# A fused attention block: five exponentials per slot of the main output projection, kept in 23 more tiles, and four PSUM banks shared by that projection and the maxima

## The chip, the cores and the metric

The kernel runs on one core of a Trainium2 chip. The metric is the time of one execution on the device in microseconds (us). TensorE (PE) multiplies and writes PSUM banks; VectorE (DVE), ScalarE (ACT) and GpSimd (POOL) work on SBUF and PSUM; SyncE (SP) issues most DMA transfers, in program order.

## The reference

```python
x = A_x                                   # 1 x 2048 x 512, fp32
xn = (x - mean) / sqrt(var + 1e-5)        # over the last axis
q, k, v = xn @ wqkv                       # 32 heads of 16
p = softmax(q @ k.T * 16 ** -0.5)         # per head, 2048 x 2048
s = (p @ v, heads side by side) @ wo
h = max(xn @ w1 + b1, 0) ** 2             # 1792 wide
g = silu(h @ w2 + b2)
return x + s * g
```

## The kernel before

Every fp32 product of the dense parts is made of three matmuls of split values (high times high, high times low, low times high). The attention is 512 slots. A unit is four heads with 512 queries; unit u takes slots 16u to 16u+15, one block of 128 keys (kb) in each. A slot makes one score tile for each of the four heads, and these go through an exp on ScalarE; two slots later four matmuls of them with v (32 output rows each, L401) add into the unit's bank `po`.

Score matmuls and the dense ones use 64 rows of the TensorE array, so two run side by side, one on each row half. In a slot one half has the dense work of the MLP or of a projection, and the other the maxima and the score matmuls; the next slot swaps the halves. The text calls one matmul on each half a round.

A unit's exps need its row maxima first, since they are subtracted inside the score matmul (two extra rows of the q tile hold the shift). So each unit's scores are made twice: 64 matmuls L317 whose tiles VectorE reduces (L324), 24 slots ahead of the unit, and later those for the exps (L1201). When the 64 are done, `max_end` notes a slot from which the shift is formed (`late`, six slots later); `shift` makes it (L368 to L371), stores it (L377, one slot later) and loads it into the rows of the q tile (L392).

PSUM has three banks for exps (`se`), three for maxima (`pm_t`), one for dense work (`pd_t`) and one for `po`. `tile` pools hand them out in turn: who writes a bank again waits for the reader of what was there. Exp results go to a ring of 17 tiles `pt`.

A unit's output leaves in steps counted in slots (`evac`; EVAC_LAST for units 29 on): the row sums are loaded into another shape (L419), inverted, stored (L428), loaded back to all rows (L433, `hl<-r_d`), GpSimd multiplies and splits (L439), and four stores (L448) put it into `on_d`, from which the projection loads its input (L677, `oc<-on_d`).

The output projection has two parts. The main part (`wo_part`, slots 454 to 485) makes 16 tiles of 128 x 512 over heads 0 to 23, two slots each, nine dense matmuls on each half; a tile is multiplied by g, x is added, and the sum goes to `sp_d` or stays in SBUF. The last part (`wo_last`, slots 486 to 510) does heads 24 to 31 for 12 tiles, three dense matmuls a slot, beside the exps of units 30 and 31; slot 502 has no dense work. Slot 494 starts on the tiles that need unit 29's output, slot 503 on those of unit 30. The four tiles that need unit 31 are made after slot 511 (`unit_final`). From slot 486 on (LAST_MAX) no maxima are left and exps take turns in the banks of both pools.

The order on TensorE is as the code writes it. Within a slot a string gives what stands beside the dense matmuls on the other half, `s` an exp's and `m` a maximum's:

```python
order = "s" * len(ex) if spare else {0: "smsmsmsm", 1: "smsmssm"}[k]
if not spare and post is None:
    if k == 0:
        order = "msmsmsms"
```

SyncE's transfers are issued in one queue in the order of the slots in which `later(n, ...)` places them; one that waits holds all behind it.

## Time and profile before

| | |
|---|---|
| time, median of 3 runs | 1630.25 us (1628.72 to 1631.37) |
| the profiled execution | 1627.99 us, span 1626.2 us |
| mean granted TensorE clock | 0.999 |
| TensorE busy | 1610.3 us of the span (99%) |
| VectorE, ScalarE, GpSimd busy | 84%, 73%, 32% |
| DMA | 208.16 MB, 128 GB/s over the span |

A row of an engine's timeline has the start in us, the time from the start of its first instruction to the end of its last, engine, line, operation, output<-inputs, tile and number of merged instructions; in brackets the idle time ahead of it and what ended that. A matmul's own time overlaps the next one's. SPq is SyncE's queue: the time at which it issues a transfer. A row of the windows' view has the stretch, then its length and for PE, PE's weight loads, DVE, ACT, POOL the busy time (and instructions), then the granted clock, the DMA engines' busy share and GB/s.

### The profile page before, as it was taken

The page shows a single profiled execution, that of the slowest core. Times are in us where ns is not written, and L with a number is a line of the kernel's source. Part 1 is how long each engine was busy: PE and PEld are TensorE (multiplying, and loading weights), DVE is VectorE, ACT ScalarE, POOL GpSimd, SP SyncE. Part 2 cuts the span into 40 slices and gives each one's busy share as a digit, 9 for nine tenths or more (in the row PEclk, how much of TensorE's full clock was granted, in tenths as well). Part 3 has the DMA queues.
Part 4 walks back from the last instruction along what each step waited for, and adds up shares of the span by engine and source line. Part 5 has one row for each costly group of instructions (what it writes and reads, how often), then busy time and mean ns, then how long its engine had stood idle before and what let it go on. Part 6 is the DMA issues. An engine that isn't in the chain of part 4 may idle for free.

```text
span 1626.2 us, 36026 instructions
## 1 busy us (share of the span) xinstructions
PE 1610.3 (99%) x13656; PEld 936.1 (58%) x13656; DVE 1362.1 (84%) x2359; ACT 1188.9 (73%) x2349; POOL 520.5 (32%) x547
## 2 busy tenths in 40 slices
PE   8999999999999999999999999999999999999998
PEld 6899665556545654664466456545654565445543
DVE  6486888888888888888888888888888888887744
ACT  7212777777777777877777777777777777777786
POOL 6436667133113310321133112311331133226421
PEclk9999999999999999999999999999999999999999
DMA  8877556434343333434343334423542252247564
GB/s 297 235 236 233 175 162 157 127 96 128 81 103 96 103 88 90 127 87 110 83 119 93 85 87 130 112 68 83 141 112 67 70 155 78 55 126 210 188 179 150
DMA packets 163565, 208.16 MB, mean 128 GB/s; under 512 B 59168, under 2 KB 79136, under 8 KB 161824
## 3 DMA queue, kind: packets, MB, share of 16 engines
q1 hardware_dynamic: 163104, 205.33, 44.6%
q8 instruction: 108, 1.77, 0.5%
q14 instruction: 65, 0.53, 0.1%
q10 hardware_dynamic: 288, 0.52, 0.1%
HBM read 148.64 MB, written 55.56 MB: 126 GB/s over the span
## 4 chain that ended last, share of the span: by engine, by line
PE 98%; DVE 1%; DMA 0%; issue 0%; SPq 0%; DVEq 0%; ACT 0%; ACTq 0%
PE po L401 31%; PE pd_t L255 20%; PE pm_t L317 16%; PE se L1201 14%; PE pd_t L223 7%; PE pm_t L1077 4%; PE pd_t L1077 1%; PE se L1047 1%; PE se L981 1%; PE se L317 1%; PE pm_t L1163 0%; PE pd_t L1047 0%; DVE mx L324 0%; DMA xt<-in_A_x_dram 0%; PE pm_t L1201 0%; PE po L981 0%
## 5 line engine op out<-in xcount | busy, mean ns | idle before, releaser
L324 DVE TENSOR_REDUCE mx<-pm_t 128x1 f32<-128x512 f32 x1927 | 1197.3, 684 | 166.9 <-PE pm_t L317 74.0
L1213 ACT ACTIVATE pt<-se 128x512 f32<-128x512 f32 x1996 | 1035.5, 614 | 252.8 <-PE se L1201 210.4
L317 PE MATMUL pm_t<-ka,qm 64*128 64x512 f32 x1927 | 769.6, 420 | 0.0
L1201 PE MATMUL se<-qe,ka 64*128 64x512 f32 x1996 | 673.0, 396 | 0.3 <-ACT pt L1213 0.3
L401 PE MATMUL po<-pt,v 128*32 128x512 f32 x4096 | 545.3, 604 | 0.2 <-DVE tsm L795 0.2
L317 PEld LDWEIGHTS pm_t<-ka,qm 64*128 64x128 f32 x1927 | 338.3, 184 | 237.0 <-DVE mx L324 225.5
L1201 PEld LDWEIGHTS se<-qe,ka 64*128 64x128 f32 x1996 | 337.2, 184 | 18.1 <-ACT pt L1213 1.7
L255 PEld LDWEIGHTS pd_t<-xc,w1s 64*128 64x128 f32 x2352 | 292.0, 186 | 82.2 <-issue 82.2
L255 PE MATMUL pd_t<-xc,w1s 64*128 64x256 f32 x2352 | 332.2, 288 | 0.0
L255 PE MATMUL pd_t<-w2t,hT 64*128 64x512 f32 x1080 | 300.6, 410 | 0.0
L255 PEld LDWEIGHTS pd_t<-w2t,hT 64*128 64x128 f32 x1080 | 179.0, 184 | 83.2 <-issue 75.5
L555 POOL TENSOR_TENSOR r<-r 128x512 f32<-128x512 f32 x56 | 58.2, 1039 | 370.3 <-ACT r L552 370.3
L401 PEld LDWEIGHTS po<-pt,v 128*32 128x32 f32 x4096 | 81.0, 108 | 159.9 <-issue 136.8
L574 POOL TENSOR_TENSOR u<-u,b_t 128x512 f32<-128x512 f32 x16 | 20.6, 1289 | 320.2 <-ACT u L573 286.3
L324 DVE TENSOR_REDUCE mx<-se 128x1 f32<-128x512 f32 x121 | 77.9, 686 | 26.0 <-PE se L317 26.0
L439 POOL TENSOR_TENSOR ot<-ot,hl 128x512 f32<-128x512 f32 x30 | 38.6, 1286 | 173.9 <-DMA hl<-r_d 132.7
L223 PE MATMUL pd_t<-wot,oc 64*128 64x512 f32 x336 | 90.2, 405 | 0.4 <-issue 0.3
L552 ACT ACTIVATE r<-pd_t,b_t 128x256 f32<-128x256 f32 x112 | 47.0, 470 | 57.0 <-PE pd_t L255 53.8
L223 PEld LDWEIGHTS pd_t<-wot,oc 64*128 64x128 f32 x336 | 58.4, 184 | 46.9 <-ACT pt L1213 12.6
L1077 PE MATMUL pm_t<-xT,wr_t 64*128 64x512 f32 x408 | 73.8, 388 | 0.0
L97 POOL TENSOR_TENSOR hT<-r,hT 128x512 fp32r<-128x512 f32 x56 | 72.3, 1291 | 4.7
L223 PE MATMUL pd_t<-w2t,hT 64*128 64x512 f32 x264 | 68.8, 393 | 0.0
(134 smaller groups left out, 1148.4 us busy)
## 6 DMA issues: line engine op xcount, KB each, us to landing
w1s<-w_d SPq DMA_DIRECT2D x196, 256.0 KB
qm<-q_d SPq DMA_DIRECT2D x384, 32.0 KB
ka<-k_d SPq DMA_DIRECT2D x96, 128.0 KB
qe<-q_d SPq DMA_DIRECT2D x384, 32.0 KB
q_d<-hl SPq DMA_DIRECT2D x16, 512.0 KB
g<-g_d SPq DMA_DIRECT2D x32, 256.0 KB
k_d<-hl SPq DMA_DIRECT2D x15, 512.0 KB
hl<-r_d SPq DMA_DIRECT2D x30, 256.0 KB
```

The lines of the kernel that those rows point to most:

```text
L97: (lo or nc.gpsimd).tensor_tensor(dst[1], raw, dst[0].bitcast(F32), op=ALU.subtract)
L223: mm = nc.tensor.matmul(out_, lh(r), rh(r), start=first_ and lane == 0, stop=last_ and lane == 1, skip_group_check=True,)
L255: mm = nc.tensor.matmul(out_, lh(r), rh(r), start=first_ and lane == 0, stop=last_ and lane == 1, skip_group_check=True,)
L317: nc.tensor.matmul(ps, qms[u][p][64 * j : 64 * j + 64, qb * P : (qb + 1) * P], kas[qd, p][64 * j : 64 * j + 64, kc * 512 : (kc + 1) * 512] ...
L324: return nc.vector.tensor_reduce(mxs[u][:, c, kc : kc + 1], ps, axis=AX.X, op=ALU.max)
L401: nc.tensor.matmul(po[32 * j : 32 * j + 32, :], vs[qd][:, (4 * kb + j) * VW : (4 * kb + j) * VW + 32], pts[j], start=(kb == 0), stop=(kb = ...
L439: nc.gpsimd.tensor_tensor(ot, ot, hl[:, 1].bitcast(F32), op=ALU.mult)
L552: nc.scalar.activation(r[:, i], ps[:, i * CW : (i + 1) * CW], AF.Relu, bias=b1_t[:, fo : fo + 1])
L555: nc.gpsimd.tensor_tensor(r, r, r, op=ALU.mult)
L1077: mm = nc.tensor.matmul(out_, lh(r), rh(r), start=first_ and lane == first, stop=last_ and lane != first, skip_group_check=True,)
L1201: nc.tensor.matmul(se, kas[qd, j // 2][b : b + 64, kb * P : (kb + 1) * P], qes[u][j // 2][b : b + 64, :], start=True, stop=True,)
L1213: return nc.scalar.activation(pts[j], se, AF.Exp, scale=0.25)
```

## The change

From slot 454 on (RUN) `run_ahead` picks the exps of a slot: all that are next in order up to a number, five in a main slot (six are allowed in slots 484 and 485), three in the tail, as long as the unit's shift is there and a `pt` tile is free. To hold what runs ahead the ring gets 23 more tiles: 3 in space left free, 18 in a new pool and 2 in a tile of v that is no longer used. For this room part of the projection's input `oc` lies in tiles of the k ring (`rot["ka"]`), the sums of the third 512 rows go through `sp_d` as well, and small tiles share space. The shifts of units 29, 30 and 31 are formed 6, 6 and 5 slots earlier (slots 451, 469 and 485 instead of 456, 474 and 490). While the main part runs, its tile is no longer `pd_t` alone: `bank()` turns four banks (three `pm_t`, one `pd_t`) between the tile and the maxima. In EVAC_LAST the load back is one slot later, and two loads of projection input move. The end has its subtractions on GpSimd and one sum on TensorE and ScalarE.

```diff
@@ -32 +32 @@
+NXR = 18
 EVAC = (1, 6, 7, 9, 11, 14)
-EVAC_LAST = (1, 3, 4, 5, 7, 9)
+EVAC_LAST = (1, 3, 4, 6, 7, 9)
...
 LAST_MAX = 486
+RUN = 454
 PAIR = (484, 485)
@@ -331 +333 @@
-                late.append((g + (8 if u == 3 else 6 if u else 0), u))
+                late.append((g + {0: 0, 3: 8, 29: 0, 30: 0, 31: 1}.get(u, 6), u))
@@ -382 +384 @@
+                shifted[u] = now[0]
             later(1, keep)
-            later(2 if u else 6, back)
+            later(4 if u == NU - 1 else 2 if u else 6, back)
...
+        shifted = {}
@@ -645 +649 @@
             tp = tail["p"] = right(wstk, "tailp", 1)
+            for tt in range(4):
+                tail[3, tt] = tp.tile([P, D], F32, name=f"ts{tt}")
+            left = ph.enter_context(tc.tile_pool(name="xpl", bufs=1))
+            more = [left.tile([P, 512], F32, name=f"xl{i}") for i in range(3)]
+            pool = right(wstk, "xpr", 1)
+            more += [pool.tile([P, 512], F32, name=f"xr{i}") for i in range(NXR)]
+            more += [vs["tiles"][0][:, 512 * i : 512 * i + 512] for i in range(2)]
+            rot["pt"] = more + rot["pt"]
             wos["oc3"] = right(o3, "oc3p", 2)
...
@@ -669 +679 @@
+                two = rot["ka"][c % 2].rearrange("p (i k n) -> p i k n", i=2, k=2)
+                one = wos["oc3"].tile([P, 2, 512], F32R, name="oc")
...
             else:
@@ -705 +717 @@
-            elif c < 2:
+            elif c < 3:
                 t = wos["f"].tile([P, D], F32, name="s")
...
+        def bank():
+            mine = wos["banks"]
+            n = next(n for n, t in enumerate(mine) if t is not wos["tile"] and t is not wos["next"])
+            mine.append(mine.pop(n))
+            return mine[-1]
         def wo_part():
+            wos["banks"] = [pm.tile([P, 512], F32, name="pm_t") for _ in range(3)]
+            wos["banks"].append(pd.tile([P, 512], F32, name="pd_t"))
+            last_bank = wos["banks"][2]
+            wos["tile"] = wos["next"] = None
             for c in range(4):
@@ -724 +746 @@
-                    ps = pd.tile([P, D], F32, name="pd_t")
+                    wos["next"] = None
+                    if k < 15:
+                        ps = bank()
+                    else:
+                        ps = last_bank
+                        wos["banks"].sort(key=lambda t: t is last_bank)
+                    wos["tile"] = ps
...
                     g, xr = wos.pop(k)
-                    if c > 1:
-                        s = tail[c, tt] = tail["p"].tile([P, D], F32, name=f"ts{c}{tt}")
+                    if c == 3:
+                        s = tail[c, tt]
                     else:
@@ -736 +764 @@
-                        if c < 2:
+                        if c < 3:
...
-                    yield from halves(wo_terms(ps, wos["t", c], tt, [0, 1, 2]), (9,), post, 1)
+                    for n, part in enumerate(halves(wo_terms(ps, wos["t", c], tt, [0, 1, 2]), (9,), post, 1)):
+                        if k == 14 and n:
+                            wos["next"] = last_bank
+                        yield part
+            wos["banks"] = None
@@ -749 +781 @@
-                if k == 18:
-                    wo_load(1, [3])
+                if k == 17:
+                    later(3, lambda: wo_load(1, [3]))
@@ -785 +817 @@
+            return ot
+        def unit_scale(po, i, rows, sm):
...
+            nc.vector.reciprocal(sm, rows[:, :, DH])
+            nc.vector.transpose(
+                ot.rearrange("p (b r) -> p b r", r=32), sm[:, :, None].to_broadcast([P, 8, 32])
+            )
+            nc.vector.tensor_tensor(ot, po[:, 256 * i : 256 * i + 256], ot, op=ALU.mult)
@@ -842 +883 @@
+            both = pe.tile([P, 512], F32, name="se")
+            nc.tensor.matmul(both, ident, parts[1][1], start=True, stop=False)
...
             for i in range(2):
-                ot = unit_back(i, *unit_turn(po, i))
-                hl = tail["p"].tile([P, 2, 256], F32R, name=f"thl{i}")
+                ot = unit_scale(po, i, *unit_turn(po, i))
+                hl = tail["e"].tile([P, 2, 256], F32R, name=f"thl{i}")
                 nc.scalar.activation(hl[:, 0], ot, AF.Copy)
+                nc.gpsimd.tensor_tensor(hl[:, 1], ot, hl[:, 0].bitcast(F32), op=ALU.subtract)
...
-            def low(i):
-                nc.vector.tensor_tensor(
@@ -867 +905 @@
-            def add(tt, a, b, eng, queue):
+            def add(tt, eng):
                 g, s = parts[tt]
-                eng.tensor_tensor(g[:, a:b], g[:, a:b], s[:, a:b], op=ALU.add)
...
-            low(0)
-            for tt, n in ((0, 0), (0, 1), (1, 0), (1, 1), (0, 2), (1, 2)):
-                out(tt, n)
-            low(1)
-            for tt in (2, 3):
-                for n in range(3):
-                    out(tt, n)
-            gate(0)
-            add(0, 0, D, nc.gpsimd, nc.scalar)
-            gate(1)
-            add(1, 0, D, nc.gpsimd, nc.scalar)
-            gate(2)
-            gate(3)
-            add(2, 0, D, nc.vector, nc.sync)
-            add(3, 0, D, nc.vector, nc.sync)
+                eng.tensor_tensor(g, g, s, op=ALU.add)
...
+            for i in range(2):
+                for tt, n in ((0, 0), (0, 1), (1, 0), (1, 1), (0, 2), (1, 2)):
+                    out(2 * i + tt, n)
+            for tt in range(4):
+                gate(tt)
+            nc.tensor.matmul(both, ident, parts[1][0], start=False, stop=True)
+            nc.scalar.activation(parts[1][0], both, AF.Copy)
+            add(0, nc.gpsimd)
+            add(2, nc.gpsimd)
+            add(3, nc.vector)
@@ -1195 +1234 @@
             if spare:
-                se = pm.tile([P, 512], F32, name="pm_t")
+                se = bank() if wos.get("banks") else pm.tile([P, 512], F32, name="pm_t")
             else:
@@ -1427 +1466 @@
                     wos["q6"] = right(wstk, "q6p", 1)
-                    later(3, lambda: load_q6(3))
+                    tail["e"] = right(wstk, "endp", 1)
+                    later(10, lambda: load_q6(3))
                 yield from wo_last(c)
...
         odd = itertools.chain((0,) * 4, itertools.cycle((1, 0)))
+        ahead_of = {}
+        def run_ahead(st, lane, n, need):
+            got = []
+            at = ahead_of.setdefault(lane, 2 * (st - 1))
+            live = sum(len(d) for d in pts.values())
+            while at < 2 * NU * 16:
+                kb, j = at // 2, lane + 2 * (at % 2)
+                if j not in pts.setdefault(kb, {}):
+                    if kb > need and (
+                        len(got) >= n or st < shifted.get(kb // 16, st) + 2 or live + len(got) > len(rot["pt"]) - 3
...
+                        break
...
+                    got.append((kb, j))
+                at += 1
+            ahead_of[lane] = at
+            return got
         flip = [0]
@@ -1442 +1501 @@
             spare = st >= LAST_MAX
+            if st < RUN:
+                todo = [
+                    (kb, j) for kb in (kb0, kb0 + 1) for j in (1 - lane, 3 - lane) if j not in pts[kb]
+                ]
+            else:
+                n = 3 if spare else 6 if st in PAIR else 5
+                todo = run_ahead(st, 1 - lane, n, st - 1)
             ex = [
-                lambda j=j, kb=kb: exp_mm(kb, j, pts[kb], spare and next(odd))
-                for kb in (kb0, kb0 + 1) for j in (1 - lane, 3 - lane) if j not in pts[kb]
+                lambda j=j, kb=kb: exp_mm(kb, j, pts[kb], (spare or st in PAIR) and next(odd))
+                for kb, j in todo
             ]
@@ -1460 +1526 @@
-            if spare and lane == 0:
-                own.append(lambda: exp_mm(kb0, 0, pts[kb0], next(odd)))
...
-            mx = [] if spare else [lambda: max_mm(1 - lane) for _ in range(2 if st in PAIR else 4 - k)]
+            mx = [] if spare else [
+                lambda: max_mm(1 - lane, bank if wos.get("banks") else None)
+                for _ in range(2 if st in PAIR else 4 - k)
+            ]
             order = "s" * len(ex) if spare else {0: "smsmsmsm", 1: "smsmssm"}[k]
...
                 if k == 0:
-                    order = "msmsmsms"
+                    order = "ssmsmsmms" if len(ex) == 5 else "msmsmsms"
                 elif lane and k == 1 and to_block:
                     order = "smsmsms"
+            elif k == 0 and not spare:
+                order = "smsmsmsms" if len(ex) == 5 else order
             if st in PAIR:
-                order = "sms_s_s_m"
+                order = {5: "smss_ss_m", 6: "smsss_ssm"}.get(len(ex), "sms_s_s_m")
+            while order.count("s") > len(ex):
+                order = order[: order.rindex("s")] + order[order.rindex("s") + 1 :]
...
             other[-1:-1] = [None] * (len(own) - len(other))
@@ -1532 +1603 @@
-            pts[st] = {}
...
-                exp_mm(st, j, pts[st], next(odd))
+            last = st == NU * 16 - 1
+            todo = [run_ahead(st, lane, 0, st if last else st - 1) for lane in range(2)]
+            for pair in itertools.zip_longest(*todo):
+                for kb, j in filter(None, pair):
+                    exp_mm(kb, j, pts[kb], next(odd))
...
```

TensorE in an even main slot (456, the first half of a projection tile; `pd_t` is that tile or its bank, `se` an exp's bank, a `pm_t` a maximum's; the number behind a name is the buffer), before and after:

```order
L223 MATMUL pd_t_21592<-wot_20339,oc_21438 128x512
L317 MATMUL pm_t_21603<-ka2_734,qm0_204 128x512
L223 MATMUL pd_t_21592<-wot_20339,oc_21438 128x512
L1201 MATMUL se_21607<-qe1_737,ka3_735 128x512
L223 MATMUL pd_t_21592<-wot_20339,oc_21438 128x512
L317 MATMUL pm_t_21611<-ka2_734,qm0_204 128x512
L223 MATMUL pd_t_21592<-wot_20339,oc_21438 128x512
L1201 MATMUL se_21615<-qe0_736,ka2_734 128x512
L223 MATMUL pd_t_21592<-wot_20339,oc_21438 128x512
L317 MATMUL pm_t_21619<-ka2_734,qm0_204 128x512
L223 MATMUL pd_t_21592<-wot_20339,oc_21438 128x512 x2
L1201 MATMUL se_21624<-qe1_737,ka3_735 128x512
```

```order
L319 MATMUL pm_t_21542<-ka2_734,qm0_204 128x512
L225 MATMUL pd_t_21545<-wot_20339,ka0_207 128x512
L1240 MATMUL se_21647<-qe1_737,ka3_735 128x512
L225 MATMUL pd_t_21545<-wot_20339,ka0_207 128x512
L319 MATMUL pm_t_21543<-ka2_734,qm0_204 128x512
L225 MATMUL pd_t_21545<-wot_20339,ka0_207 128x512
L1240 MATMUL se_21654<-qe0_736,ka2_734 128x512
L225 MATMUL pd_t_21545<-wot_20339,oc_21475 128x512
L319 MATMUL pm_t_21544<-ka2_734,qm0_204 128x512
L225 MATMUL pd_t_21545<-wot_20339,oc_21475 128x512
L319 MATMUL pm_t_21542<-ka2_734,qm0_204 128x512
L225 MATMUL pd_t_21545<-wot_20339,oc_21475 128x512
```

Before, each maximum takes a bank of a pool of three in turn and one half round is empty at the end (x2). After, the last maximum uses the buffer of the first one of the slot (21542), two others lie between, and a fifth exp follows in the last round.

SyncE's queue at the seam of the main part and the tail (`sm` are a unit's sums, `r_d` its reciprocals, `sh_d31` unit 31's shift, `g` and `s` the inputs of a tile's end), before and after:

```order
L428 DMA r_d29_126<-sm_22797 128x16
L433 DMA hl_22959<-r_d29_126 128x1x512
L704 DMA g_22965<-g_d_136 128x512
L710 DMA s_22967<-sp_d_133 128x512
L704 DMA g_23014<-g_d_136 128x512
L710 DMA s_23016<-sp_d_133 128x512
L777 DMA q63_23042<-on_d3_132 64x2x512 x2
L761 DMA out_0_dram<-g_22801 128x512
L448 DMA on_d3_132<-hl_22959 16x2x512 x4
L704 DMA g_23068<-g_d_136 128x512
L710 DMA s_23070<-sp_d_133 128x512
L677 DMA oc_23075<-on_d3_132 128x2x512
```

```order
L432 DMA r_d29_126<-sm_22783 128x16
L379 DMA sh_d31_96<-sh_22925 128x64
L716 DMA g_22940<-g_d_136 128x512
L722 DMA s_22942<-sp_d_133 128x512
L437 DMA hl_22962<-r_d29_126 128x1x512
L716 DMA g_22985<-g_d_136 128x512
L722 DMA s_22987<-sp_d_133 128x512
L396 DMA qe2_738<-sh_d31_96 2x16x32 x2
L396 DMA qe3_739<-sh_d31_96 2x16x32 x2
L793 DMA out_0_dram<-g_22787 128x512
L452 DMA on_d3_132<-hl_22962 16x2x512 x4
L716 DMA g_23034<-g_d_136 128x512
```

The load of the reciprocals (`hl<-r_d29`) stood right behind their store; now the store of unit 31's shift and a `g` and an `s` stand between them. The load of q for the end (`q63`) has left this place.

TensorE in slot 511, ahead of its matmuls with v, before and after:

```order
L1201 MATMUL pm_t_23585<-qe2_738,ka2_734 128x512
L1201 MATMUL se_23588<-qe2_738,ka2_734 128x512
L1201 MATMUL pm_t_23591<-qe3_739,ka3_735 128x512
L1201 MATMUL se_23594<-qe3_739,ka3_735 128x512
L401 MATMUL po_23306<-pt16_1494,v1_1789 32x512
```

```order
L1240 MATMUL pm_t_23474<-qe3_739,ka3_735 128x512
L1240 MATMUL se_23477<-qe3_739,ka3_735 128x512
L1240 MATMUL pm_t_23480<-qe2_738,ka2_734 128x512
L1240 MATMUL se_23483<-qe2_738,ka2_734 128x512
L1240 MATMUL pm_t_23486<-qe3_739,ka3_735 128x512
L1240 MATMUL se_23489<-qe3_739,ka3_735 128x512
L1240 MATMUL pm_t_23492<-qe2_738,ka2_734 128x512
L1240 MATMUL se_23495<-qe3_739,ka3_735 128x512
L405 MATMUL po_23231<-pt12_1490,v1_1789 32x512
```

Four exps stood there, now eight.

35 lines of the change are left out of this document (19 added, 16 removed).

## The prediction

> **What bounds the kernel now.** I read the page first (busy shares, the chain that ended last), then TensorE's timeline in a slot of the main output projection and in the tail, then the DMA queue's and GpSimd's timelines round the seam between the two.
>
> ```profile
> span 1626.2 us, 36026 instructions
> PE 1610.3 (99%) x13656; PEld 936.1 (58%) x13656; DVE 1362.1 (84%) x2359; ACT 1188.9 (73%) x2349; POOL 520.5 (32%) x547
> PE 98%; DVE 1%; DMA 0%; issue 0%; SPq 0%; DVEq 0%; ACT 0%; ACTq 0%
> ```
>
> TensorE is busy for 99% of the span and holds 98% of the chain: a gain has to take rounds away from it (a round is one matmul on each row half), and every wait in its queue is paid in full. The profiled execution took 1627.99 us, 1.7 above its span; the median of the runs is 1630.25. I work out a difference against the profiled execution and add it to the median.
>
> TensorE's timeline in one main slot, and the busy time of two stretches (all main slots, the tail's first slot):
>
> ```profile
> 1480.95 0.50 PE L223 MATMUL pd_t<-wot,oc 64*128 64x512 f32 x1
> ...
> 1482.67 0.62 PE L223 MATMUL pd_t<-wot,oc 64*128 64x512 f32 x2
> 1483.22 1.07 PE L401 MATMUL po<-pt,v 128*32 128x512 f32 x8
> 1484.22 0.49 PE L223 MATMUL pd_t<-wot,oc 64*128 64x512 f32 x1
> ```
> ```profile
> 1454.80:1559.33 104.53, 104.53 (x800) 58.57 (x796) 79.03 (x135) 77.48 (x149) 52.16 (x45) 1.00 0.64 198
> 1559.33:1562.01 2.68, 2.40 (x21) 0.83 (x17) 0.25 (x2) 2.08 (x5) 2.51 (x2) 1.00 0.94 249
> ```
>
> In the slot the nine projection matmuls run from 1480.95 to 1483.29 at a pitch of 0.23 us (the last two: 0.62 with one of 0.39), then the attention matmuls take 1.00: 3.27 in all. The 32 main slots take 104.53, 3.267 each, so none of them waits. Nine projection matmuls stand against eight others (four exps, four maxima): the ninth round has a free half. The tail slots:
>
> ```profile
> 1592.98 0.49 PE L1201 MATMUL pm_t<-qe,ka 64*128 64x512 f32 x1
> ...
> 1594.64 0.49 PE L223 MATMUL pd_t<-w,hl 64*128 64x512 f32 x1
> ...
> 1596.76 0.49 PE L223 MATMUL pd_t<-w,hl 64*128 64x512 f32 x1
> ...
> 1598.65 0.49 PE L223 MATMUL pd_t<-w,hl 64*128 64x512 f32 x1
> ```
>
> A tail slot of four rounds takes 2.12, one of three 1.89, the slot with no projection 1.66.
>
> **What moves, and its sum.** Call S the start of slot 486 (1559.33 before).
>
> *Main slots: 0 in rounds, +2.0 in waits.* The fifth exp fills the free half, so the nine rounds stay. But the exps share three banks as before, and the projection's bank now comes out of the same four as the maxima, which leaves these three too. What a handed-back bank costs:
>
> ```profile
> 1559.93 0.61 ACT pt L1213
> 1560.58 0.49 PE se L1201
> ```
> ```profile
> 1461.35 0.49 PE L317 MATMUL pm_t<-ka,qm 64*128 64x512 f32 x1
> ...
> 1461.91 2.48 DVE L324 TENSOR_REDUCE mx<-pm_t 128x1 f32<-128x512 f32 x4 [0.55 <-PE pd_t L223]
> ```
>
> An exp of 0.61 ends at 1560.54, the matmul that wants its bank starts at 1560.58 and lasts 0.49 where a flowing one takes 0.39: in effect 0.14 after the release. A maximum written until 1461.84 is reduced from 1461.91; four in 2.48 is one every 0.60, 0.68 each. In an even slot after the change (projection tile begun) the exps stand in rounds 0, 1, 3, 5, 8 and the maxima in 2, 4, 6, 7. Round k starts at 0.34 + 0.23(k-1). The exp of round 5 needs the bank of round 0's: matmul to 0.50, exp to about 1.15, usable at 1.29 against 1.26. The maximum of round 7 needs the bank of round 2's: written until 0.96, reduced 1.03 to 1.71, usable at 1.85 against 1.72 (1.75 with the first delay). Together about 0.13 to 0.15 late. In an odd slot the same pairs are six rounds apart and nothing is late. The even slots 454 to 478 carry five exps: 13 x 0.15 = 2.0. Ends: 0 (a weight load may run ahead of the matmul and swallow it) and 3.3 (0.25 each). I take the worked value.
>
> *The first tail slots: +3.3.* The output of unit 29 is what slot 494 multiplies. In the trace:
>
> ```profile
> 1421.32 0.53 SPq L433 DMA_DIRECT2D hl<-r_d  x1
> ...
> 1557.25 0.55 SPq L433 DMA_DIRECT2D hl<-r_d  x1
> 1557.85 0.47 SPq L704 DMA_DIRECT2D g<-g_d  x1
> ...
> 1558.90 0.58 SPq L704 DMA_DIRECT2D g<-g_d  x1
> ...
> 1561.94 1.29 SPq L777 DMA_DIRECT2D q<-on_d  x2
> ...
> 1567.14 1.73 SPq L448 DMA_DIRECT2D on_d<-hl  x4
> ...
> 1570.75 0.37 SPq L677 DMA_DIRECT2D oc<-on_d  x1
> ...
> 1572.47 0.43 SPq L377 DMA_DIRECT2D sh_d<-sh  x1
> ```
> ```profile
> 1426.06 1.29 POOL L439 TENSOR_TENSOR ot<-ot,hl 128x512 f32<-128x512 f32 x1 [9.90 <-DMA hl<-r_d]
> ...
> 1563.44 1.28 POOL L439 TENSOR_TENSOR ot<-ot,hl 128x512 f32<-128x512 f32 x1 [1.52 <-DMA hl<-r_d]
> ```
> ```profile
> 1576.53 0.47 PE L223 MATMUL pd_t<-wot,oc 64*128 64x512 f32 x1 [0.25 <-issue]
> ```
>
> The load of the reciprocals is issued at 1557.25; 6.19 later GpSimd starts on them; 3.70 later the four stores; 3.61 after these the load of oc, which waits for them; 5.78 later TensorE starts slot 494, having stood 0.25. The chain is 19.28 from end to end, and before it just suffices: slot 494 starts at S+17.20. After, the shift of unit 31 is formed right after the last maximum, and its store stands ahead of the reciprocals' load in the one queue, followed by g and s. The queue is served in order, so the load can't leave before that shift exists:
>
> ```profile
> 1559.20 0.22 DVE L332 TENSOR_REDUCE m<-mx 128x16 f32<-128x64 f32 x1
> ...
> 1569.00 0.20 DVE L368 STREAM_TRANSPOSE tr<-m 128x32 f32<-128x32 f32 x1
> ...
> 1569.45 0.19 DVE L371 SCALAR_TENSOR_TENSOR sh<-tr,sh 128x32 fp32r<-128x32 f32 x1
> ```
>
> The maxima of unit 31 end at 1559.42, the three small operations take 0.64: S+0.73. One store (0.43) and two loads (1.05 for g and s, from 1557.85 to 1558.90) later the reciprocals' load leaves at S+2.3, against S-2.08 before. With the same 19.28 slot 494 starts at S+21.5. Its own time without a wait is 8 x 1.89 = S+15.1, so TensorE stands some 5 us, and nothing behind that matmul can pass. Two of the loads that ran beside this chain (q, 512 KB, at 1561.94) now come ten slots later; at the 249 GB/s of that stretch they were 2.1 us of transfer. I give half of it back: S+20.5, so +3.3. Ends: a reciprocals' load in an empty queue (issued 1421.32, used at 1426.06: 4.74) and the full 2.1 less on the last load give S+18.0, +0.8; the 19.28 and one more microsecond for the two loads now ahead give S+22.5, +5.3.
>
> The Trainium skill ("DMA: Bandwidth & Descriptors", Anatomy of one DMA) fits one DMA to 2.0 us plus its bytes at 436 GB/s. For 256 KB that is 2.6 against the 6.19 and 4.74 of the rows; with it for both loads the chain would be 13.1 and slot 494 would start 0.3 after its own time; by it the sum would be -1.0 and the time 1629.2, which is the second rival below. The rows of this trace differ from it by a factor of two, and they decide.
>
> *From slot 494 to 511: -2.5.* The inputs of slot 503, and slot 498:
>
> ```profile
> 1584.67 0.50 PE L223 MATMUL pd_t<-wot,oc 64*128 64x512 f32 x1
> ```
> ```profile
> 1589.61 1.81 SPq L830 DMA_DIRECT2D hl<-on_d  x4
> ```
>
> Before 1576.53 to 1610.69, 34.16. After: sixteen slots of three rounds, 30.24, and slot 502, empty of exps, about 0.9 (a group of attention matmuls alone): 31.1. Slot 503 needs the four loads at 1589.61, 4.94 after slot 498 began (1584.67); with the 3.61 that four such transfers need they land at 8.55, where four slots and the gap leave 8.46: with the start of the matmul 0.4 of waiting. 31.6. Ends -3.0 and -2.0. Here the rounds moved to the main slots pay: eight slot pairs of 4.01 become 3.78, and before's own short waits in slots 486 to 494 are part of the term above.
>
> *The last slot: +1.9.* It now holds eight exps, with nothing but them to hide behind.
>
> ```profile
> 1610.69 0.49 PE L1201 MATMUL pm_t<-qe,ka 64*128 64x512 f32 x1
> ...
> 1611.22 0.60 ACT L1213 ACTIVATE pt<-pm_t 128x512 f32<-128x512 f32 x1
> ...
> 1611.36 3.03 PE L401 MATMUL po<-pt,v 128*32 128x512 f32 x24
> ...
> 1612.67 0.62 ACT L1213 ACTIVATE pt<-se 128x512 f32<-128x512 f32 x1
> ...
> 1614.42 0.45 DVE L789 STREAM_TRANSPOSE tt<-po 128x256 f32<-128x256 f32 x1 [3.21 <-PE po L401]
> ```
>
> Four exps start from 1611.22 to 1612.67, one every 0.48. Eight: the last starts at 0.53 + 7 x 0.48 = 3.89 after the slot, ends at 4.53. From the end of the last exp (1613.29) to the transposition 1.13: 5.66 against 3.73. Ends +1.7 and +2.1.
>
> *The end: -0.6.* GpSimd takes the two remainders off VectorE, TensorE and ScalarE one of the sums.
>
> ```profile
> 1622.46 0.93 SPq L873 DMA_DIRECT2D out_dram<-g  x2
> ```
>
> The last store ends at 1623.39, 8.97 after the first transposition. After, VectorE has one sum behind its four gates instead of two, 0.6 less. Ends -1.0 and 0.
>
> ```profile
> SPq L433 <- DMA r_d<-sm: 3.8, 1, 3.8
> ```
>
> At nothing: four more stores and four more loads of intermediate sums, some 0.45 of queue each, covered by the queue's standing still, here 3.8 ahead of the reciprocals' load; without that cover 3.6 of issue, which would reach TensorE only through slot 494. The w splits moved back on GpSimd (32% busy) are used only from slot 503 on. Unit 29's shift goes ahead of the first loads of the projection's input in the same queue: 0 to 0.6, the three small operations, once, in the range.
>
> Sum: +2.0 + 3.3 - 2.5 + 1.9 - 0.6 = **+4.1 us**, 1632.1 for a profiled execution, 1634.3 on the median.
>
> **The rivals.** *The chain lands sooner.* Slot 494 at S+18 instead of S+20.5: +1.6, 1631.9. For it: the 4.74 row, the emptier queue. Against it: two loads now stand just ahead. 24%. *No wait at slot 494 at all, not slower.* If oc is there by S+15.1 the term becomes -2.1 and the sum -1.3: 1629.0; if the even slots wait for nothing as well, -3.3, 1627.0: with the good ends of the other terms (-0.9 together) this is the only way I see past the 0.2%. It needs the chain to take 12.8 instead of 19.28; no row has it so short. 18%. *The banks weigh more.* Odd slots wait too, or the late maxima push on into the next slot: 0.25 in each of 26 slots is 6.5 instead of 2.0, 1638.9. Against it: VectorE has 0.8 us free in each slot (2.48 of 3.27). 10%.
>
> **How the numbers follow.** The forecast has 48%. About 0.2% (3.3 us) is what a measurement here tells from no change. Slower by more: the forecast and the heavier banks, 58%. Within: the sooner chain, and a quarter of the second rival (banks that wait as worked out), 28%. Faster by more: the rest of it, 14%. The ends of the terms add up to -4.2 (with no wait at slot 494) and +9.9; together they are unlikely, so the range goes from 1627.5 to 1639.5, which leaves out the fast end of the second rival and the worst of the third.
>
> **What would show it.** Right: even main slots of about 3.4, odd of 3.27; the reciprocals' load some 2.3 after slot 486 begins; TensorE standing several microseconds ahead of slot 494's first projection matmul; tail slots of 1.89; eight exps in the last slot and 5.6 from its start to the transposition. Wrong: slot 494 without a wait, or main slots still at 3.27 throughout. The forecast falls if oc lands before S+18.

## The result and the profile after

The changed kernel takes 1644.05 us (median of six runs, 1640.83 to 1646.74) against 1629.70 before: ratio 1.0085, 95% interval 1.0072 to 1.0099. It is slower, as forecast, but by 14.35 us instead of 4.1, outside the range. The profiled executions differ by 14.6 (spans 1640.8 and 1626.2).

From the page after, the busy shares and the chain that ended last:

```profile
PE 1617.1 (99%) x13660; PEld 944.2 (58%) x13660; DVE 1363.4 (83%) x2356; ACT 1191.3 (73%) x2350; POOL 523.1 (32%) x549
...
PE 93%; DMA 2%; DVE 2%; issue 1%; SPq 1%; POOL 1%; ACT 0%; POOLq 0%; ACTq 0%
```

TensorE still counts as 99% busy, but its part of the chain fell from 98% to 93%: transfers, VectorE and the queue now stand in it. The windows' view, by stage (main slots; slots 486 to 493; 494 to 510; from 511 on):

```profile
1455.68:1566.78 111.10, 108.19 (x828) 60.71 (x824) 79.73 (x132) 89.30 (x174) 52.14 (x45) 1.00 0.67 201
1566.78:1589.23 22.45, 15.78 (x114) 5.37 (x111) 8.34 (x16) 11.75 (x22) 5.73 (x5) 0.91 0.57 151
1589.23:1623.64 34.41, 33.96 (x232) 11.38 (x232) 14.40 (x32) 24.96 (x48) 2.81 (x4) 0.91 0.67 225
1623.64:1640.80 17.16, 11.81 (x64) 5.75 (x60) 7.31 (x14) 5.75 (x12) 4.03 (x4) 0.97 0.21 77
```

| stage | before | after | difference | forecast |
|---|---|---|---|---|
| up to slot 454 | 1454.80 | 1455.68 | +0.9 | 0 |
| main slots | 104.53 | 111.10 | +6.6 | +2.0 |
| slots 486 to 493 | 17.20 | 22.45 | +5.25 | +3.3 |
| slots 494 to 510 | 34.16 | 34.41 | +0.25 | -2.5 |
| slot 511 to the first transposition | 3.73 | 5.76 | +2.0 | +1.9 |
| from there to the end | 11.8 | 11.4 | -0.4 | -0.6 |

The 0.9 us ahead of slot 454 are there by the end of unit 2 (its copy starts at 306.6 before and 307.6 after), in code that the change leaves as it is; I count them as the difference of two executions (in the other traces of the changed kernel and its versions slot 454 begins between 1454.62 and 1456.60). Two waits of TensorE stand out of the rest, slot 462 in the main part and slot 494:

```profile
1487.01 0.49 PE L225 MATMUL pm_t<-wot,oc 64*128 64x512 f32 x1 [2.58 <-DMA oc<-on_d]
...
1589.23 0.76 PE L225 MATMUL pd_t<-wot,oc 64*128 64x512 f32 x1 [6.18 <-DMA oc<-on_d]
```

Both wait for a load of the projection's input. (Slot 491 also takes 2.99 instead of 1.89; in five runs with the same order of the queue the row there names the rows of unit 31's shift, `qe<-sh_d`. Here the wait at slot 494 hides it.) SyncE's queue, where it issued the shifts of units 29 and 31 and these loads:

```profile
1452.78 0.34 SPq L379 DMA_DIRECT2D sh_d<-sh  x1
1453.16 0.95 SPq L689 DMA_DIRECT2D ka<-on_d  x2
...
1477.53 0.47 SPq L689 DMA_DIRECT2D oc<-on_d  x1
...
1568.30 0.32 SPq L379 DMA_DIRECT2D sh_d<-sh  x1
...
1569.67 0.53 SPq L437 DMA_DIRECT2D hl<-r_d  x1
...
1583.62 0.37 SPq L689 DMA_DIRECT2D oc<-on_d  x1
```

In the kernel before, the first block of these loads and the last one for slot 462:

```profile
1449.49 2.94 SPq L677 DMA_DIRECT2D oc<-on_d  x6
...
1474.23 0.47 SPq L677 DMA_DIRECT2D oc<-on_d  x1
```

The load for slot 494 is what the prediction described: the reciprocals' load leaves 2.89 after slot 486 begins (1566.78), behind unit 31's shift, and 19.56 later slot 494 starts. The wait in slot 462 it had not. Behind slot 494 the granted clock falls (windows; the wait, slots 494, 495, and two more):

```profile
1581.10:1589.23 8.13, 1.96 (x18) 0.66 (x15) 1.39 (x2) 1.83 (x4) 0.00 (x0) 0.75 0.81 208
1589.23:1592.67 3.44, 3.44 (x14) 1.06 (x14) 0.16 (x1) 1.58 (x3) 0.00 (x0) 0.50 1.06 409
1592.67:1595.80 3.13, 3.13 (x18) 1.03 (x14) 1.35 (x2) 1.58 (x3) 0.00 (x0) 0.56 1.06 268
1595.80:1599.59 3.79, 3.79 (x33) 1.30 (x30) 1.00 (x4) 2.91 (x6) 0.00 (x0) 1.00 0.76 264
```

At this clock slots 494 and 495 take 6.57 instead of 3.78: 2.8 us that are in none of the prediction's terms. An even and an odd main slot, and slot 470:

```profile
1520.06:1523.49 3.43, 3.43 (x31) 2.01 (x28) 2.40 (x4) 2.94 (x6) 2.58 (x2) 1.00 0.79 189
1523.49:1526.78 3.29, 3.29 (x32) 1.82 (x28) 2.57 (x5) 2.69 (x6) 0.00 (x0) 1.00 0.74 250
...
1512.67:1516.77 4.10, 3.78 (x30) 2.01 (x26) 4.00 (x9) 3.04 (x6) 2.57 (x2) 1.00 0.70 234
```

Even slots take about 0.15 more than odd ones. Slot 470 takes 0.66 more than other even ones; on VectorE one of the small operations of unit 30's shift (L373) stands there, and GpSimd works on a tile's end at the same time:

```profile
1513.08 0.18 DVE L372 TENSOR_SCALAR sh<-tr 128x32 fp32r<-128x32 f32 x1
1513.30 1.17 DVE L373 SCALAR_TENSOR_TENSOR sh<-tr,sh 128x32 fp32r<-128x32 f32 x1
```
```profile
1513.12 1.29 POOL L765 TENSOR_TENSOR s<-s,g 128x512 f32<-128x512 f32 x1 [4.06 <-ACT s L764]
```

L373 takes 0.19 elsewhere; here it ends just behind GpSimd's operation. Last, slot 511 (1623.64), its eighth exp on ScalarE and the transposition:

```profile
1627.12 0.66 ACT L1252 ACTIVATE pt<-pm_t 128x512 f32<-128x512 f32 x1
```
```profile
1629.40 0.45 DVE L821 STREAM_TRANSPOSE tt<-po 128x256 f32<-128x256 f32 x1 [5.24 <-PE po L405]
```

### The profile page after: what moved, and what is told of

Same layout as the page of the kernel before. It is cut to its first block, busy times and chain, and to the rows that moved or that the text cites. A ratio compares the mean times of both kernels' runs of the same rounds, so it can differ in the third digit from the quotient of the medians.

```text
span 1640.8 us, 36030 instructions
## 1 busy us (share of the span) xinstructions
PE 1617.1 (99%) x13660; PEld 944.2 (58%) x13660; DVE 1363.4 (83%) x2356; ACT 1191.3 (73%) x2350; POOL 523.1 (32%) x549
## 4 chain that ended last, share of the span: by engine, by line
PE 93%; DMA 2%; DVE 2%; issue 1%; SPq 1%; POOL 1%; ACT 0%; POOLq 0%; ACTq 0%
PE po L405 30%; PE pd_t L257 20%; PE pm_t L319 16%; PE se L1240 13%; PE pd_t L225 4%; PE pm_t L1116 4%; PE pd_t L1116 1%; PE pm_t L225 1%; PE se L1086 1%; PE se L1020 1%; DMA oc<-on_d 1%; DVE mx L326 1%; PE se L319 1%; DMA xr<-in_A_x_dram 0%; DMA g_d<-u 0%
## 5 line engine op out<-in xcount | busy, mean ns | idle before, releaser
L326 DVE TENSOR_REDUCE mx<-pm_t 128x1 f32<-128x512 f32 x1897 | 1180.5, 684 | 162.5 <-PE pm_t L319 76.1
L1252 ACT ACTIVATE pt<-se 128x512 f32<-128x512 f32 x1893 | 976.6, 613 | 237.3 <-PE se L1240 199.2
L319 PE MATMUL pm_t<-ka,qm 64*128 64x512 f32 x1897 | 756.5, 420 | 0.6 <-DVE mx L326 0.6
L405 PE MATMUL po<-pt,v 128*32 128x512 f32 x3820 | 521.8, 605 | 0.0
L319 PEld LDWEIGHTS pm_t<-ka,qm 64*128 64x128 f32 x1897 | 332.7, 184 | 238.2 <-DVE mx L326 227.1
L405 PEld LDWEIGHTS po<-pt,v 128*32 128x32 f32 x3820 | 77.4, 108 | 148.1 <-issue 125.7
L1116 PEld LDWEIGHTS pm_t<-xT,wr_t 64*128 64x128 f32 x408 | 60.7, 185 | 0.0
L1252 ACT ACTIVATE xr<-se 128x512 f32<-128x512 f32 x89 | 48.0, 614 | 13.8 <-PE se L1240 12.6
```

What stands on the lines that cost most here:

```text
L319: nc.tensor.matmul(ps, qms[u][p][64 * j : 64 * j + 64, qb * P : (qb + 1) * P], kas[qd, p][64 * j : 64 * j + 64, kc * 512 : (kc + 1) * 512] ...
L326: return nc.vector.tensor_reduce(mxs[u][:, c, kc : kc + 1], ps, axis=AX.X, op=ALU.max)
L405: nc.tensor.matmul(po[32 * j : 32 * j + 32, :], vs[qd][:, (4 * kb + j) * VW : (4 * kb + j) * VW + 32], pts[j], start=(kb == 0), stop=(kb = ...
L1116: mm = nc.tensor.matmul(out_, lh(r), rh(r), start=first_ and lane == first, stop=last_ and lane != first, skip_group_check=True,)
L1252: return nc.scalar.activation(pts[j], se, AF.Exp, scale=0.25)
```

## The experiments

My theory after the result: the order of SyncE's queue costs most (slots 462 and 494), standing still lowers the clock on top of it, and the banks and the last slot cost what was forecast. The main rival is bandwidth: more transfers in a shorter time, so that loads land late whatever their order. One execution of the changed kernel lies anywhere between 1640.8 and 1646.7, so a single time can't tell 2 us; the slots in the trace can.

**The reciprocals' load ahead of unit 31's shift.**

```diff
-EVAC_LAST = (1, 3, 4, 6, 7, 9)
+EVAC_LAST = (1, 3, 4, 5, 7, 9)
```

> Only EVAC_LAST is put back to the old steps, so the load of unit 29's reciprocals stands ahead of the store of unit 31's shift in SyncE's queue. Queue theory: the load leaves about 1561.3 instead of 1569.7 of the profile after the change, the chain of 19.6 us from there ends near S+14 (S the start of slot 486), less than the eight tail slots need (15.1), so slot 494 starts without a wait, the clock stays at 1.00 behind it and slots 494 and 495 take 1.89 instead of 3.44 and 3.13. Gain 7.3 + 2.8 = about 10 us: 1634. Bandwidth rival (the added spills and the closer loads make the transfers slow, whatever their order): the load still needs 7 us and more, slot 494 still waits several us, gain under 3 us: above 1641.

Measured 1636.28, ratio to before 1.0048 (1.0031 to 1.0064), so some 8 us under the changed kernel. Slots 486 to 493, then 494 to 510:

```profile
1567.69:1583.83 16.14, 15.20 (x116) 5.18 (x112) 7.56 (x16) 11.63 (x22) 6.03 (x5) 1.00 0.70 202
1583.83:1615.43 31.60, 31.14 (x232) 10.60 (x232) 14.39 (x32) 24.92 (x48) 2.80 (x4) 1.00 0.73 246
```

22.45 became 16.14 (0.94 us of wait is left) and 34.41 became 31.60, with the clock at 1.00: 9.1 us, all from one step of one number. (The time fell by less, since slot 462 took 6.78 in this execution and the clock fell behind it.) From the reciprocals' load, which left at 1565.40, to slot 494 it is 18.43: the transfers are hardly faster, they start sooner. So the order of the queue decides at slot 494, and bandwidth is not what the change adds there.

**Unit 29's shift later.** Five steps of the `late` list later, then six as in the kernel before; the first run showed that five left the store in front of the second block of loads. (Steps 0 and 1 fall into the same slot, so that all three shifts of the change are five slots earlier; the "6, 6 and 5" of its description count steps.)

```diff
-late.append((g + {0: 0, 3: 8, 29: 0, 30: 0, 31: 1}.get(u, 6), u))
+late.append((g + {0: 0, 3: 8, 29: 6, 30: 0, 31: 1}.get(u, 6), u))
```

> Only unit 29's shift is formed five slots later (slot 456), so its store no longer stands in the queue ahead of the first loads of the projection's input; unit 29's first exps don't stand before slot 462 either way. Queue theory: these loads leave near 1449.5 + 0.9 as in the kernel before instead of 1453.2, the queue is some 3 us earlier at the later loads, and the 2.6 us for which TensorE stands in slot 462 go away: main slots 108.4 instead of 111.1, time 1641.3. Rival (the loads of slot 462 are slow because of bandwidth: 9.4 us for the last of them): the wait in slot 462 stays within 1 us of 2.6, time 1644.

> The changed kernel with unit 29's shift alone put back by the full six slots (the run with five slots left its store ahead of the second block of loads, 2.5 us of standing at 1459.9, and its four loads ahead of the last two). Now the queue has the order of the kernel before up to slot 462. Queue theory: the last load for slot 462 is issued near 1475.2 instead of 1477.5 and lands by 1484, when the slot wants it (1482.7 + 1.4): the slot takes 3.44 to 3.8 instead of 6.2, time about 1641. Bandwidth rival: it lands 9 us after its issue and the slot keeps a wait of 1.5 us or more.

1639.79 and 1642.36. With five, slot 462 took 5.24 instead of 6.19; with six, 6.99. The expectation was missed. Yet with six TensorE stood 1.59 instead of 2.58 there; the slot was longer because the clock fell behind the wait. And the wait has another name:

```profile
1484.77 0.54 PE L1240 MATMUL se<-qe,ka 64*128 64x512 f32 x1 [1.59 <-DMA qe<-sh_d]
```

With five exps a slot since 454, unit 29's first exp stands in slot 462, two slots ahead of the unit, and now it is the rows of the late shift that aren't there. The load itself, issued at 1475.95, landed at 1484.50, some 0.3 after TensorE would have wanted it; in the changed kernel it came 2.75 late. So nearly all of that wait came from the early store, and the early shift can't simply be taken back: early it delays the loads of slot 462, late it delays that slot's exps.

**The small loads behind.** The 13 loads of projection rows in `wo_small` stand ahead of the last two loads for slot 462.

```diff
-            later(3, wo_small)
+            later(8, wo_small)
```

> The changed kernel with one thing moved: the 13 small loads of projection rows (0.46 us of queue each, 1467.0 to 1475.9 in the changed kernel), which stand ahead of the last two loads for slot 462, are issued five slots later, behind those loads. Unit 29's shift stays early. Queue theory: the last load for slot 462 leaves some 6 to 8 us sooner (near 1470) and lands well ahead of 1484: the wait of 2.6 us in slot 462 is gone, time 1641 to 1641.5. Bandwidth rival: with the same bytes in flight the load lands as late as before and the wait stays.

1641.05. The last load leaves at 1468.40 instead of 1477.53 (queue), and slot 462 waits for nothing (first window); the second window is slot 474:

```profile
1468.40 0.63 SPq L689 DMA_DIRECT2D oc<-on_d  x1
...
1479.04 0.55 SPq L666 DMA_DIRECT2D ts<-in_A_wo_dram  x1
1485.43 0.33 SPq L672 DMA_DIRECT2D ts<-in_A_wo_dram  x1
```
```profile
1481.85:1485.29 3.44, 3.44 (x31) 2.03 (x27) 2.40 (x4) 2.94 (x6) 2.93 (x3) 1.00 0.03 12
1523.32:1529.32 6.00, 3.75 (x32) 1.94 (x28) 2.52 (x5) 3.14 (x6) 2.53 (x2) 1.00 0.68 234
```
```profile
1484.87 0.53 POOL L669 MEMSET ts<- 128x512 f32 x1
```

The bandwidth rival falls at slot 462 too, as what decides that wait; that loads are slow is true all the same (this one took 10.2 us from issue to landing, and was early enough). But the small loads now wait for a memset that stands late on GpSimd; the queue stands from 1479.59 to 1485.43, and slot 474, with unit 30's first exps, waits 2.3 us for the rows of that shift. The wait moved.

**The banks.** The even slots in the odd slots' order, the finished tile's bank used third instead of first:

```diff
-                    order = "ssmsmsmms" if len(ex) == 5 else "msmsmsms"
+                    order = "smsmsmsms" if len(ex) == 5 else "msmsmsms"
...
+                        old = wos["tile"]
                         ps = bank()
+                        if old is not None:
+                            wos["banks"].remove(old)
+                            wos["banks"].insert(2, old)
```

> Even main slots get the order of the odd ones (exps in rounds 0, 2, 4, 6, 8, maxima in 1, 3, 5, 7), and the bank of the tile just finished becomes the third of the maxima's turn instead of the first, since ScalarE copies it until 0.37 us into the slot. Bank theory: no bank is wanted again in under six rounds, even slots take 3.28 instead of 3.44: 13 x 0.16 = 2.1 us less, main slots 109.0, time 1642. Rival (ScalarE, with five exps and half a copy a slot, sets the pace): even slots stay at 3.40 and more, or odd ones lengthen by as much.

Even slots take 3.28, the odd ones as before (row: an even slot), except slot 483, of which more below. ScalarE is not what sets the pace. The one time was 1643.23: slot 462 took 8.78 in that execution, 3.68 of it waiting, and the clock fell behind the wait.

```profile
1528.47:1531.75 3.28, 3.28 (x30) 1.83 (x26) 2.48 (x5) 2.92 (x6) 2.56 (x2) 1.00 0.85 299
```

And no sharing at all: the tile keeps its bank, the maxima their three.

```diff
-            wos["banks"] = [pm.tile([P, 512], F32, name="pm_t") for _ in range(3)]
-            wos["banks"].append(pd.tile([P, 512], F32, name="pd_t"))
...
+                    ps = pd.tile([P, 512], F32, name="pd_t")
```

> The changed kernel without the sharing of banks: the projection's tile keeps its one bank and the maxima their three, five exps as they are. ScalarE's copy of a finished tile ends 0.37 us into the next even slot (1519.78 + 0.65 against 1520.06), and the new tile's first matmul now needs that bank: even slots 0.4 to 0.5 longer, besides the 0.16 of the third exp's bank; 16 x 0.45 = 7 us, main slots 118 instead of 111, time 1651. Rival (sharing costs more than it saves): even slots of 3.4 or less, time at or under 1644.

1645.28. An odd slot with the wait behind it, and an even one:

```profile
1525.84:1529.55 3.71, 3.37 (x32) 1.82 (x28) 2.58 (x5) 3.05 (x6) 0.00 (x0) 1.00 0.77 217
1529.55:1532.97 3.42, 3.42 (x26) 1.92 (x26) 2.39 (x4) 2.56 (x5) 2.58 (x2) 1.00 0.78 198
```

The pair takes 7.13 against 6.72 with shared banks: the wait of 0.4 for ScalarE's copy is there, as expected for each pair, some 5 us in 13 pairs. (The sum of 7 in the expectation took 16; the last three, with four exps, have none.) Sharing is a gain for five exps. The 0.15 in each even slot is not its price: without sharing even slots still take 3.42, and in the odd slots' order 3.28, so it comes from the order.

**Four exps in four of the last tail slots.**

```diff
-                n = 3 if spare else 6 if st in PAIR else 5
+                n = 4 if st in (503, 505, 507, 509) else 3 if spare else 6 if st in PAIR else 5
```

> The changed kernel with four exps instead of three in slots 503, 505, 507 and 509, so that four instead of eight are left to slot 511. Each of the four slots becomes 0.23 longer (2.12), the last one goes from 5.65 to about 3.7, as in the kernel before (3.63): -1.9 + 0.9 = -1.0 us, time 1643. If the last slot is held by something other than its exps it stays above 5.

Slots 503 to 510, then slot 511:

```profile
1610.89:1626.94 16.05, 16.05 (x120) 5.89 (x117) 5.66 (x12) 14.32 (x28) 0.00 (x0) 1.00 0.71 240
1626.94:1630.57 3.63, 3.63 (x32) 1.18 (x28) 0.52 (x1) 2.31 (x5) 0.00 (x0) 1.00 0.19 72
```

8 x 1.89 = 15.1 became 16.05, slot 511 3.63 instead of 5.65: 1.1 us, as expected. The time, 1644.47, hides it: slot 462 took 7.78, with a wait of 2.62 (2.58 in the changed kernel's profile), but this time the clock fell behind it.

**Standing still in the kernel before.** Unit 29's store and the load behind it later, in the kernel before the change:

```diff
-EVAC_LAST = (1, 3, 4, 5, 7, 9)
+EVAC_LAST = (1, 3, 4, 7, 9, 11)
...
-                    wo_load(1, [3])
+                    later(3, lambda: wo_load(1, [3]))
```

> The kernel before, with unit 29's output stored three to two slots later in EVAC_LAST and the load of it for slot 494 behind that store; nothing else. By the chain of that kernel (store behind unit 31's shift, 1570 to 1572, load of oc 4 us later, 5.8 us until its use) TensorE should stand some 4 to 5 us ahead of slot 494. If standing still is what lowers the clock, the rows behind slot 494 show granted clock under 1.00 for some microseconds, as after the 6.2 us in the changed kernel; if it is the changed kernel's load that lowers it, the clock stays at 1.00 here. Time 1634 without, 1637 with a lowered clock.

1637.55. TensorE stands 6.01 ahead of slot 494, and the clock falls behind it (the wait's slot, slot 494, the next ones):

```profile
1576.75:1584.72 7.97, 1.96 (x19) 0.67 (x16) 1.38 (x2) 2.46 (x6) 0.00 (x0) 0.78 0.61 197
1584.72:1588.34 3.62, 3.62 (x18) 1.42 (x18) 0.16 (x1) 2.56 (x5) 0.00 (x0) 0.54 0.77 295
1588.34:1592.00 3.66, 3.66 (x34) 1.53 (x30) 1.54 (x3) 2.78 (x6) 0.00 (x0) 1.00 0.09 33
```

So the clock falls without the change as well; and with the change, but only 0.94 of waiting at this slot (the run with the reciprocals' load moved), it stayed at 1.00. It is the standing still, not the change's own load.

**All repairs together**, in four steps. The first has unit 29's shift six slots later and unit 30's one, the even slots' order, the four exps, and unit 29's reciprocals made earlier in the queue:

```diff
-EVAC_LAST = (1, 3, 4, 6, 7, 9)
+EVAC_LAST = (1, 3, 3, 4, 7, 9)
...
-                        wo_ask(16)
-                        wo_ask(17)
...
+                        if k == 15 and n:
+                            wo_ask(16)
+                            wo_ask(17)
```

> All repairs together: unit 29's shift six slots later, unit 30's one slot later (past GpSimd's work on a tile, during which one of its small operations took 1.17 instead of 0.19 us), unit 29's reciprocals made, stored and loaded ahead of the loads for the tail and of unit 31's shift, the even slots in the order of the odd ones, four exps in slots 503, 505, 507 and 509. By rows: main slots 32 x 3.28 + 0.9 = 106 (104.5 before), slots 486 to 493 at 1.89 = 15.1 (17.2), slots 494 to 510 31.6 + 0.9 = 32.5 (34.2), last slot 3.7 (3.6), the end 0.4 shorter: together 2.6 us under the kernel before, about 1627. If something else of the change costs time (bandwidth, ScalarE) it stays above 1631.

1629.69, ratio 1.0008 (0.9998 to 1.0018), 2.7 above what was expected. Main slots, 486 to 493, 494 to 510:

```profile
1455.97:1564.72 108.75, 106.84 (x826) 58.76 (x822) 80.09 (x135) 89.19 (x175) 52.16 (x45) 1.00 0.67 198
1564.72:1579.84 15.12, 15.12 (x114) 5.13 (x110) 6.97 (x16) 11.37 (x22) 6.04 (x5) 1.00 0.82 233
1579.84:1612.39 32.55, 32.09 (x240) 11.33 (x236) 14.99 (x33) 27.17 (x53) 2.81 (x4) 1.00 0.73 240
```

Both tail stages are as worked out; the main slots keep 2.0 in slot 462 (the shift's rows), 0.3 each in slots 466 and 483, and 0.8 in slot 470, where unit 30's shift still met GpSimd: one slot later on the list was the same slot in the program.

In the next two, five exps begin at slot 458 instead of 454, so that unit 29's first exps stand in slot 463, and unit 30's shift is formed a slot later; the first of them moves the small loads as well.

```diff
-RUN = 454
+RUN = 458
...
-                late.append((g + {0: 0, 3: 8, 29: 6, 30: 1, 31: 1}.get(u, 6), u))
+                late.append((g + {0: 0, 3: 8, 29: 6, 30: 2, 31: 1}.get(u, 6), u))
...
-            later(3, wo_small)
+            later(8, wo_small)
```

> The version with all repairs, changed in three places: the small loads stand behind the loads for slot 462; five exps a slot begin at slot 458 instead of 454, so that unit 29's first exps stand two slots later than 462, where they waited 1.9 us for the rows of its shift in two runs; unit 30's shift is formed one slot later still (its small operation took 1.17 us again beside GpSimd). Against the run with all repairs: -2.0 in slot 462, -0.8 in slot 470, the rest alike, so 2.8 less than 1629.7: 1626.9, 0.1% under the kernel before (1628.7). If the moved loads delay others, or the exps given up at 454 to 457 come back at the end (0.12 each, 8 of them: 1.0), it stays at 1628 or above.

1635.69, ratio 1.0038 (1.0024 to 1.0052), instead of a gain: slot 474 waits 6.4 us for unit 30's rows, behind the queue held by the memset. The next has the same without the last two lines of that diff:

> The version with all repairs (1629.7), now with the small loads in their old place again (five slots later they held the queue for 6.3 us behind a memset of GpSimd), five exps a slot from slot 458 on instead of 454, and unit 30's shift one slot later. The same 4 exps stay for slot 511. Unit 29's first exps stand in slots 463 and 464, when the rows of its shift have landed (1485.0 in that run, slot 463 at 1485.7): the 1.9 us of slot 462 go, of which the last load for that slot (landed 0.4 late there) keeps up to 0.4; slot 470 gives 0.8 back. 1629.7 - 2.5 = 1627.2. If another wait takes their place, 1629 and more.

1629.21, ratio 1.0005 (0.9996 to 1.0014): slots 462 and 470 take 3.28, slot 474 waits 2.25 for unit 30's rows. Last, that shift back by one slot (`30: 1`):

> The last version with unit 30's shift put one slot earlier again: in that version its first exps waited 2.3 us for the shift's rows in slot 474 (6.01 instead of 3.28). One slot earlier the slot 470 takes 0.8 more, as in the first version with all repairs, where slot 474 waited for nothing. 1629.2 - 2.7 + 0.8 = 1627.3, 0.1% under the kernel before; if the shift's rows come late in any case, 1629 as it was.

1628.61 against 1629.04, ratio 0.9996 (0.9987 to 1.0006), the same as before within what can be told. The four stages of the profiled execution (1626.81, the lowest of eleven):

```profile
1455.18:1561.69 106.51, 106.17 (x827) 59.18 (x823) 80.09 (x135) 88.92 (x175) 52.27 (x45) 1.00 0.68 203
1561.69:1577.36 15.67, 15.19 (x115) 5.18 (x111) 7.45 (x16) 11.62 (x22) 5.99 (x5) 1.00 0.74 215
1577.36:1609.88 32.52, 32.07 (x236) 11.35 (x236) 14.42 (x33) 26.92 (x52) 2.81 (x4) 1.00 0.72 242
1609.88:1625.00 15.12, 10.08 (x60) 5.08 (x56) 7.31 (x14) 3.75 (x8) 4.00 (x4) 0.95 0.23 87
```

Against before: main slots +2.0, slots 486 to 493 -1.5, 494 to 510 -1.6, the end -0.4. So with every large wait gone, two thirds of what is saved in the tail (3.1) are eaten by what stays in the main slots: 0.8 in slot 470, 0.5 in slot 483, 0.1 each in slots 466 and 482, and some 0.01 in each slot; what is left is too little to be told in the times. Slot 483 is a price of the even slots' repair: there the next tile's bank is already kept free, and by the new turn of the banks the four maxima have two left, used one after the other. VectorE in that slot:

```profile
1552.13 0.69 DVE L326 TENSOR_REDUCE mx<-pd_t 128x1 f32<-128x512 f32 x1 [0.87 <-PE pd_t L319]
1552.74 0.68 DVE L326 TENSOR_REDUCE mx<-pm_t 128x1 f32<-128x512 f32 x1
1553.41 0.69 DVE L326 TENSOR_REDUCE mx<-pd_t 128x1 f32<-128x512 f32 x1
1554.02 0.68 DVE L326 TENSOR_REDUCE mx<-pm_t 128x1 f32<-128x512 f32 x1
```

The third maximum waits until the first one's bank is read (TensorE starts it at 1552.88). In the changed kernel, whose turn leaves three, slot 483 takes 3.28.

## Why the prediction was wrong

Three steps failed: half of two loads' time was given back at slot 494, the clock behind a wait was put at nothing, and the early store of unit 29's shift at 0 to 0.6. They make 7.5 of the 10.5 us between forecast and profile.

- *The direction and the place at slot 494 were right.* The queue held the reciprocals' load behind unit 31's shift, as written; moving it alone gave 9 us back. With that the two rivals in which the chain lands sooner fell: slot 494 came later than forecast, not earlier.
- *"I give half of it back: S+20.5" failed.* The chain from that load to slot 494 took 19.56, as in the kernel before (19.28); the two loads that no longer ran beside it made it no shorter (18.43 in the run with the load moved, so at most 0.9). The load left at S+2.89 instead of S+2.3, since unit 31's shift was itself 0.7 longer: its L372 took 0.90 beside GpSimd. Slot 494 came at S+22.45, the far end that I gave for it (22.5).
- *The 31.6 us from slot 494 to 511 were right, but only at full clock, and partly by luck.* The run with the load moved measured 31.60; but slot 503 did not wait the 0.4 that the sum gives it (1.89), and slot 498 took 2.42, 0.5 that the sum has not. No term stood for what the clock does behind a wait of 5 us, although the wait itself was in the sum: +2.8.
- *"Unit 29's shift goes ahead of the first loads ...: 0 to 0.6" failed.* I priced the three small operations and not the queue: the store stood 2.5 us waiting for them, all loads behind it began at 1453.16 instead of 1449.49, and a load that had landed just in time for slot 462 came 2.6 late. Nor had I looked at which slot uses that load, or at where unit 29's first exps now stand; the runs showed that both ends of this wait are tight.
- *The banks' term held, with its mechanism:* 0.15 in each even slot, nothing in odd ones, all of it from round 5 on; the run in the odd slots' order removed it, the run without sharing did not.
- *The last slot and the end held:* 2.0 for 1.9, and -0.4 for -0.6.
- Not foreseen, and small: 0.66 in slot 470.
- A slip in the working: the ends of the terms add up to -4.4 and, with the 0.6 for unit 29's shift, +9.3, not to -4.2 and +9.9. The forecast does not hang on it.

Put together, of the 10.5 us between forecast and profile 4.6 are main slots (slot 462 2.75, slot 470 0.66, the rest in pieces of 0.3 and less), 2.8 the clock, 1.95 the chain at slot 494, 0.9 the stretch ahead of the change, 0.3 the last slot and the end. What stays open: why the wait of slot 462 differs from execution to execution (2.2 to 3.7 us in the four with that order of the queue and shared banks), and why the clock falls behind some waits of that length and not behind others.

## What to carry to other kernels

A store that waits for a value formed "right away" holds everything behind it in the same queue; follow each load behind it to the slot that uses it, and ask how late it may come, before the new place is called free. When work is run ahead, its inputs are needed ahead as well, so the time by which each must land moves with it. A wait of several microseconds on TensorE costs more than itself: add what the clock takes back behind it.

## What the hardware did that I had not expected

*The clock after standing still.* In the changed kernel and the runs TensorE stood for 0.9 us or more 26 times in the part from slot 454 on. Behind the ten waits of 3.7 us and longer the granted clock fell to 0.50 each time; behind waits of 1.2 to 2.6 it did in six cases of 13, and behind the three of 1.0 and less never. A low stretch behind these waits lasts 3.41, 6.83 or 10.24 us, one, two or three times 3.41, and can begin within the wait (in the changed kernel from 1585.19 to 1595.43). A wait of 1.59 was followed by a clock of 0.54 (first row), another of 1.59, in the same slot of another version, by 1.00 (second row):

```profile
1484.77:1487.77 3.00, 3.00 (x14) 2.51 (x16) 1.24 (x2) 1.91 (x4) 2.75 (x4) 0.54 0.96 253
```
```profile
1484.54:1487.54 3.00, 3.00 (x25) 1.94 (x25) 2.26 (x4) 2.50 (x5) 2.75 (x4) 1.00 0.96 247
```

The Trainium skill ("TensorE: Matmul & The Clock Gate", Part 1) states that the clock halves after an idle window of about 3.4 us that runs freely. The long waits agree, and so do the lengths of the low stretches; the six short waits do not, so here a wait is not free of it because it is shorter than that.

*VectorE beside GpSimd.* An operation of 128 x 32 elements with its data in SBUF took 1.17 instead of 0.19 (L373, unit 30's shift, in the changed kernel and in all its versions but the two that form this shift a slot later, where it took 0.19) and 0.90 instead of 0.18 (L372, unit 31's) while GpSimd worked on a tile. Both end just behind GpSimd's operation; the second one (GpSimd's ran from 1566.73 to 1568.01):

```profile
1567.15 0.90 DVE L372 TENSOR_SCALAR sh<-tr 128x32 fp32r<-128x32 f32 x1
```

The Trainium skill ("Advanced Engine Details and Errata", VectorE Performance Modes) states that VectorE's second SBUF port is shared with GpSimd, so that GpSimd's instructions and VectorE's two-port ones block each other. The traces agree with such blocking, by up to 1.0 us for one small operation; in which mode these two ran, no trace shows.
